# One early load put behind an activation, two warming products fewer, and three steps of the first items reordered

## The chip, the cores and the metric

The kernel runs on one core of one Trainium2 chip. The metric is the device time of one execution in microseconds, the median of several runs. A core has five engines that work in parallel, each through its own list of instructions in order: PE (matrix products, with its weight loads shown as PEld), DVE and ACT (elementwise work), POOL and SP (here they mostly issue DMAs). Semaphores hold an instruction back until another engine or a DMA has got far enough. All times below are in microseconds.

## The reference

The result is a gated mix of two branches over the same input x of 2048 rows and 512 columns, in float32:

```python
g = _sigmoid((x * gate_w).sum(-1, keepdims=True))
a = Re(DFT_seq(DFT_hidden(x)))          # four matrix products with cos/sin matrices
b = (silu(x @ w1) * (x @ w3)) @ w2      # 512 -> 1376 -> 512
return g * a + (1 - g) * b
```

Branch a is written with real and imaginary matrices: `a = x @ Wd_re.T`, `b = x @ Wd_im.T`, then `Ws_re @ a - Ws_im @ b`. The change touches only the start of the first half of branch b, `silu(x @ w1)` and `x @ w3`.

## The kernel before

**Products in three parts.** PE multiplies rounded float32 numbers. To keep the accuracy, each operand is split in two: `high` (line 107) rounds it on ACT, `low` (line 110) takes the rest on DVE, and `split` (line 113) does both. Each product then takes three matmuls: high by high, high by low, low by high (`mm3`, line 117, and `half`, line 420).

**Seven products in place of eight.** Most of the kernel multiplies 2 by 2 blocks with seven block products, which need sums of blocks. x^T is loaded as four blocks per half of the rows, B11, B21, B12 and B22 (`load_xo`, line 195, the tensor `xt`), and the sums T1 to T4 (`sum_xo`, line 205) are split like the blocks. For a weight chunk of 128 columns of w1 and w3, the raw load is `ws` (`load_w`, line 221); `wa` holds the split of its first three blocks, `wu` their four sums, and `wb` the split of these.

**Items.** The work of this stage is a list of items n = 0 to 20, each a weight chunk c and one half g of the rows. Item 0 is done by hand with eight plain block products into four PSUM banks C (lines 416 to 482), so that PE can start as soon as a single block of x and a single block of weights are there. From item 1 on `gate_up(n)` (line 337) does seven block products X, Y, Z. LOOK = 3: the first two products of item n + 3 are made while item n is worked on. For item n, `copy_x` copies X to `s1` on ACT, `sum_g` (line 296) adds Y on DVE, which completes the gate's sum and releases Y's bank (`bank(4 + n % 2)`), and `gate1` (line 301) takes the Silu of it on ACT, in place.

**Order.** The schedule is manual (line 399): each engine's list has the order of the calls in the code. Lines 440 to 501 write out the start by hand. Beside that there are tables `early`, `second`, `mid` and `at_end`, to which `do(table, n, f, ...)` (line 503) adds work that `gate_up(n)` runs at the named place: `early` behind the copy of X, `second` behind the copy of Z, `mid` behind the addition into u4, `at_end` last.

**The start.** SP issues, in this order, the first of four blocks of the first weights (`load_w(0, 0, 1)`, 128 KB), block B11 of x (512 KB), the other three blocks of the first weights (384 KB; the third load), then B21, B12, B22 and three more weight chunks (512 KB each). All of them stand in SP's one queue. Meanwhile DVE clears a small tile `warm`, and PE multiplies it by itself WARM = 11 times into a bank that nothing reads: these are the warming products. ACT's first activation, a Silu of 24 columns of `warm` into `act0` (line 407), loads the table of functions. `act0` is used later (line 923) in the same way for another table.

In item 0, C[0, 0] takes B11 and then B21, C[1, 0] the same with other weights; then C[0, 1] and C[1, 1] take B12 and B22. The Silu of C[0, 0] (line 455) stands ahead of the split of B22 (line 457) in ACT's list.

Of the kernel before, what the change touches and what calls it, by code (L numbers as in the profile page):

```python
# [9 lines left out]
AF = mybir.ActivationFunctionType  # L10
# [11 lines left out]
NG = NST // 2  # L22
NC = (F + P - 1) // P
NP2 = (NC + 1) // 2
WARM = 11
LOOK = 3
K = 9
W2_AT = (9, 11, 13, 15)
# [4 lines left out]
def fnet_swiglu_gate_kernel(  # L33
# [20 lines left out]
    nc = tc.nc  # L54
# [25 lines left out]
    def bank(k, name):  # L80
        return psum.tile([P, 512], F32, tag=f"ps{k}", name=name)
# [31 lines left out]
    def split(hi, lo, src):  # L113
        high(hi, src)
        low(hi, lo, src)
# [7 lines left out]
    act0 = const.tile([P, 24], F32, tag="act0", name="act0")  # L123
# [81 lines left out]
    def sum_xo(g, k, t):  # L205
        ST[g, k] = t
        nc.vector.tensor_sub(t, *(ST[g, v] for v in SUMS[k]))

    def xo_parts(g, k):
        o = XO[g][:, :, OPS.index(k)]  # L210
        return flat_x(o[:, 0]), flat_x(o[:, 1]), ST[g, k]

    def split_xo(g, k):
        split(*xo_parts(g, k))

    WS, WA, WB = {}, {}, {}
# [4 lines left out]
    def load_w(w, lo=0, hi=4):  # L221
        if lo == 0:
            WS[w] = f4_a.tile([P, 4, 256], F32, tag=f"f4_{4 + w % (LOOK + 1)}", name=f"ws{w}")
        nc.sync.dma_start(WS[w][:, lo:hi].rearrange("p a n -> p (a n)"),  # L224
                          w13[SETS[w], :, lo * 256 : hi * 256])
# [7 lines left out]
    def wa_parts(w, lo, hi):  # L233
        return (*(flat(WA[w][:, h, lo:hi]) for h in range(2)), flat(WS[w][:, lo:hi]))
# [47 lines left out]
    def copy_x(n, x):  # L282
        s1 = s1p.tile([P, 512], F32, tag="s1", name=f"s1_{n}")
        nc.scalar.activation(s1, x, AF.Copy)
        G[n] = (x, s1)
# [5 lines left out]
    def prod2(n):  # L291
        y = bank(4 + n % 2, f"Y{n}")
        prod(y, n, 1, 1, True)
        return y

    def sum_g(n, y):
        s1 = G[n][1]
        nc.vector.tensor_add(s1, s1, y)
        put_score(n, 0, s1)

    def gate1(n):
        nc.scalar.activation(G[n][1], G[n][1], AF.Silu)
# [3 lines left out]
    def put_score(n, j, gate):  # L306


        c, g = ITEMS[n]
        if c < NC - 1:  # L310
            return
        if not SC:
            SC[0] = wide("sc")
        p = F % P - 32 * g
        t = SC[0].rearrange("p (b n) -> p b n", b=2)
        nc.scalar.activation(t[p : p + 32, j], gate[F % P :], AF.Copy)
        if j == 1:
            nc.gpsimd.dma_start(gs[2 * g : 2 * g + 2].rearrange("b o n -> o b n"), t[p : p + 1])
            if g == 1:
                at_end.setdefault(n + 1, []).append(lambda: free(SC[0]))  # L320
# [10 lines left out]
    early, second, mid, at_end = {}, {}, {}, {}  # L331
# [70 lines left out]
    warm = s1p.tile([P, 1024], mybir.dt.bfloat16, tag="s1", name="warm")[:, :512]  # L402
    nc.vector.memset(warm, 0.0)
    wps = bank(7, "wps")
    for n in range(WARM):
        nc.tensor.matmul(wps, warm[:, :P], warm, start=True, stop=True)
    nc.scalar.activation(act0, warm[:, :24], AF.Silu)
    load_w(0, 1, 4)
    for k in ("B21", "B12", "B22"):
        load_xo(0, k)  # L410
# [7 lines left out]
    C = {(i, j): bank((0, 4, 6, 7)[2 * i + j], f"C{i}{j}") for i in range(2) for j in range(2)}  # L418

    def half(i, j, w, x, start):  # L420


        wp = lambda h, sl: a21[:, h, sl] if w is None else WA[0][:, h, w, sl]
        xp = lambda q, h: b12[:, h, q * 512 : (q + 1) * 512] if x is None else XO[0][:, h, x, q, :]
        for r in range(2):
            sl = slice(r * P, (r + 1) * P)
            for n, (u, v) in enumerate(((0, 0), (1, 0), (0, 1))):
                nc.tensor.matmul(C[i, j], wp(u, sl), xp(r, v), start=start and r == n == 0,  # L428
                                 stop=not start and r == 1 and n == 2)
# [5 lines left out]
    s1 = s1p.tile([P, 512], F32, tag="s1", name="s1_0")  # L435
# [16 lines left out]
        split(*xo_half("B21", q))  # L452
    half(0, 0, 1, 1, False)
    split(b12[:, 0], b12[:, 1], ST[0, "B12"])
    nc.scalar.activation(s1, C[0, 0], AF.Silu)
    half(1, 0, 2, 1, False)
    split_xo(0, "B22")
    half(0, 1, 0, None, True)
    WS.pop(0)
    load_w(4)  # L460
# [25 lines left out]
    y2 = prod2(2)  # L486
# [5 lines left out]
    low_wb(1)  # L492
    high(*xo_parts(0, "T3")[::2])
    y3 = prod2(3)
    sum_g(2, y2)
    copy_x(3, x3)
    low(*xo_parts(0, "T3"))
    new_wa(4)
    split(*wa_parts(4, 0, 3))
    gate1(2)  # L500
    sum_xo(0, "T4", ST[0, "B21"])

    def do(work, n, f, *a):
        work.setdefault(n, []).append(lambda: f(*a))
# [2 lines left out]
    do(early, 1, lambda: low(*xo_parts(0, "T1")))  # L507
    do(second, 1, lambda: split_xo(0, "T4"))
    do(second, 1, free, *(ST[0, b] for b in ("B11", "B21", "B12", "B22")))
    do(second, 1, sum_g, 3, y3)  # L510
    do(mid, 1, gate1, 3)


    for k in ("B11", "B21", "B12", "B22"):
# [426 lines left out]
    for p in range(KD):  # L941
        early = p < NG - NP2
# [71 lines left out]
```

## Time and profile before

| what | value |
|---|---|
| median of 3 runs | 711.14 (710.78 to 711.51) |
| the profiled execution, its own time | 710.82 |
| its span, first to last instruction | 709.1 |
| mean granted TensorE clock over the span | 0.999 |
| mean DMA rate over the span | 243 GB/s |
| SP's second load (B11), issue to landing | 4.14 |
| the third load, 384 KB, issue to landing | 4.6 |

The profile is one execution. Its page gives the busy time and the number of instructions of each engine, and the chain of work that ended last: followed back from the last instruction, at each step to what released it or to the instruction ahead of it on its engine. The timeline gives instructions in order of time, equal ones merged with their count; a merged row's length is the union of its instructions, whose last one ends later than the next can start, so spacings are read from starts. "SPq" is SP's issuing of DMAs, not the transfer.

### The profile page before, as it was taken

What the parts mean: (1) busy time and instruction counts of PE and PEld (TensorE: products, weight loads), DVE (VectorE), ACT (ScalarE), POOL (GpSimd) and SP (SyncE); (2) the same over time, 40 slices, a digit from 0 to 9 for tenths busy, and PEclk for the clock granted to TensorE, in tenths of its full rate; (3) what the DMA queues carried; (4) which work ended last, traced back from release to release, by engine and by line L of the source; (5) the groups of instructions that cost most, each with busy time, mean ns of one, the idle gap of its engine ahead of it and who ended that gap; (6) DMA issues with size and microseconds to landing.
All of it is one profiled execution on the core that took longest, in us unless ns stands there. A gap on an engine that the chain in (4) does not pass through costs nothing.

```text
span 709.1 us, 8596 instructions
## 1 busy us (share of the span) xinstructions
PE 703.6 (99%) x3089; PEld 578.5 (82%) x3089; DVE 605.1 (85%) x735; ACT 369.1 (52%) x479; POOL 64.0 (9%) x118
## 2 busy tenths in 40 slices
PE   9999999999999999999999999999999999999997
PEld 6788888888888888888888888888888888888886
DVE  6989988787679999887999589969997896897985
ACT  5665555655446754454554553544455455455451
POOL 0021111121110000000110001100110000000000
PEclk9999999999999999999999999999999999999999
DMA  7575556589997566712596238915999981773932
GB/s 281 201 290 214 209 193 251 186 311 355 421 410 269 221 193 241 293 60 89 175 361 251 90 121 296 370 49 189 379 419 415 358 272 56 296 285 135 321 120 89
DMA packets 45403, 172.54 MB, mean 243 GB/s; under 512 B 5296, under 2 KB 5424, under 8 KB 41520
## 3 DMA queue, kind: packets, MB, share of 16 engines
q1 hardware_dynamic: 32464, 118.50, 46.1%
q0 software_dynamic: 12608, 52.97, 18.8%
q8 instruction: 24, 0.39, 0.2%
q10 hardware_dynamic: 288, 0.52, 0.2%
q14 instruction: 19, 0.16, 0.1%
HBM read 114.82 MB, written 57.16 MB: 243 GB/s over the span
## 4 chain that ended last, share of the span: by engine, by line
PE 99%; DMA 1%; DVE 0%; ACT 0%; SPq 0%; issue 0%
PE P L119 69%; PE X L119 16%; PE Z L119 8%; PE Y L119 4%; PE C L428 2%; DMA xs_B<-xt 1%; DVE zc L807 0%; ACT xo L108 0%; SPq L224 0%
## 5 line engine op out<-in xcount | busy, mean ns | idle before, releaser
L119 PE MATMUL P<-zo,a 128*128 128x512 f32 x1344 | 305.5, 389 | 0.0
L119 PEld LDWEIGHTS P<-zo,a 128*128 128x128 f32 x1344 | 252.0, 188 | 53.3 <-DVE zo L111 1.1
L108 ACT ACTIVATE zo<-B 128x1024 fp32r<-128x1024 f32 (+1 forms) x182 | 189.3, 1045 | 184.5 <-PE P L119 96.4
L111 DVE TENSOR_TENSOR zo<-B,zo 128x1024 fp32r<-128x1024 f32 (+1 forms) x182 | 218.0, 1206 | 48.2 <-ACT zo L108 47.3
L119 PE MATMUL P<-zo,H 128*128 128x512 f32 x468 | 106.2, 389 | 0.0
L119 PEld LDWEIGHTS P<-zo,H 128*128 128x128 f32 x468 | 87.9, 188 | 18.2
L665 DVE TENSOR_TENSOR B<-B,B 128x1024 f32<-128x1024 f32 (+1 forms) x78 | 93.1, 1194 | 0.1
L119 PE MATMUL X<-xo,wb 128*128 128x512 f32 x378 | 93.1, 390 | 0.0
L119 PEld LDWEIGHTS X<-xo,wb 128*128 128x128 f32 x378 | 70.8, 188 | 15.4 <-DVE xo L111 0.5
L119 PE MATMUL P<-zo,Y 128*128 128x512 f32 x336 | 76.3, 389 | 0.0
L119 PEld LDWEIGHTS P<-zo,Y 128*128 128x128 f32 x336 | 63.1, 188 | 13.1
L327 POOL DMA_DIRECT2D hsp<-h x42 | 23.0, 548 | 128.4 <-DVE h L379 75.6
L119 PE MATMUL Z<-xo,wb 128*128 128x512 f32 x126 | 32.0, 389 | 0.0
L119 PE MATMUL X<-xo,wa 128*128 128x512 f32 x126 | 32.0, 389 | 0.0
L119 PE MATMUL Z<-xo,wa 128*128 128x512 f32 x126 | 32.0, 389 | 0.0
L119 PE MATMUL Y<-xo,wa 128*128 128x512 f32 x126 | 32.0, 389 | 0.0
L668 DVE TENSOR_TENSOR B<-B,B 128x1024 f32<-128x1024 f32 x26 | 31.8, 1221 | 0.0
L882 ACT ACTIVATE zu<-P 128x512 f32<-128x512 f32 x32 | 19.1, 598 | 20.3 <-PE P L119 20.3
L373 DVE TENSOR_TENSOR u<-u,X 128x512 f32<-128x512 f32 x21 | 14.4, 687 | 16.4 <-PE X L119 16.4
L119 PEld LDWEIGHTS Z<-xo,wb 128*128 128x128 f32 x126 | 23.6, 188 | 5.0
L119 PEld LDWEIGHTS Z<-xo,wa 128*128 128x128 f32 x126 | 23.6, 188 | 4.9
L119 PEld LDWEIGHTS X<-xo,wa 128*128 128x128 f32 x126 | 23.6, 188 | 4.9
(135 smaller groups left out, 550.5 us busy)
## 6 DMA issues: line engine op xcount, KB each, us to landing
B<-cc SPq DMA_DIRECT2D x64, 512.0 KB, 5.9
hsp<-h POOLq DMA_DIRECT2D x42, 256.0 KB, 3.7
B<-hsp SPq DMA_DIRECT2D x20, 512.0 KB, 10.3
wbsp<-wb POOLq DMA_DIRECT2D x8, 1024.0 KB, 4.3
wb<-wbsp SPq DMA_DIRECT2D x8, 1024.0 KB, 7.7
B<-zsp SPq DMA_DIRECT2D x16, 512.0 KB, 7.6
H<-w2sp SPq DMA_DIRECT2D x6, 1024.0 KB, 8.9
ws<-w SPq DMA_DIRECT2D x11, 512.0 KB, 4.8
```

Source lines behind the costliest of these rows:

```text
L108: nc.scalar.activation(hi, src, AF.Copy)
L111: nc.vector.tensor_sub(lo, src, hi.bitcast(F32))
L119: nc.tensor.matmul(ps, u, v, start=first and n == 0, stop=last and n == 2, skip_group_check=chain)
L327: nc.gpsimd.dma_start(hsp[g, b + k, j // 2, :, j % 2 * 512 : (j % 2 + 1) * 512], h)
L373: nc.vector.tensor_add(u4, u4, x)
L428: nc.tensor.matmul(C[i, j], wp(u, sl), xp(r, v), start=start and r == n == 0, stop=not start and r == 1 and n == 2)
L665: nc.vector.tensor_add(t, t, RAW[blk, b, q][:, :n])
L668: nc.vector.tensor_sub(t, RAW[blk, "B12", q], t)
L882: nc.scalar.activation(U[name][:, r], ps[r], AF.Copy)
```

## The change

It has three parts.

1. The first activation writes its 24 columns into the tile of the first weights, at the place that the third load will fill, in place of `act0`; `act0` gets a plain copy. Since the third load writes the same place, it has to wait for the activation, and SP's later loads stand behind it. WARM goes from 11 to 9.
2. The Silu of C[0, 0] moves behind the split of B22, that is, behind its high part in ACT's list.
3. The gate sum of item 2 (`sum_g(2, y2)` on DVE) and its Silu (`gate1(2)` on ACT) move from the written-out start into item 1, to the places that item 3's had, and those of item 3 move to item 2.

```diff
-WARM = 11
+WARM = 9
...
     wps = bank(7, "wps")
     for n in range(WARM):
         nc.tensor.matmul(wps, warm[:, :P], warm, start=True, stop=True)
-    nc.scalar.activation(act0, warm[:, :24], AF.Silu)
+
+    nc.scalar.activation(WS[0][:, 1, :24], warm[:, :24], AF.Silu)
+    nc.scalar.activation(act0, warm[:, :24], AF.Copy)
     load_w(0, 1, 4)
...
     split(b12[:, 0], b12[:, 1], ST[0, "B12"])
-    nc.scalar.activation(s1, C[0, 0], AF.Silu)
     half(1, 0, 2, 1, False)
     split_xo(0, "B22")
+    nc.scalar.activation(s1, C[0, 0], AF.Silu)
     half(0, 1, 0, None, True)
...
     y3 = prod2(3)
-    sum_g(2, y2)
     copy_x(3, x3)
     low(*xo_parts(0, "T3"))
     new_wa(4)
     split(*wa_parts(4, 0, 3))
-    gate1(2)
     sum_xo(0, "T4", ST[0, "B21"])
...
-    do(second, 1, sum_g, 3, y3)
-    do(mid, 1, gate1, 3)
+    do(second, 1, sum_g, 2, y2)
+    do(mid, 1, gate1, 2)
+    do(early, 2, sum_g, 3, y3)
+    do(mid, 2, gate1, 3)
```

## The prediction

> **What bounds the kernel now.** I read the profile's page first, then the chain of work that ended last.
>
> ```profile
> span 709.1 us, 8596 instructions
> PE 703.6 (99%) x3089; PEld 578.5 (82%) x3089; DVE 605.1 (85%) x735; ACT 369.1 (52%) x479; POOL 64.0 (9%) x118
> PE 99%; DMA 1%; DVE 0%; ACT 0%; SPq 0%; issue 0%
> ```
>
> PE is the bound from its first product to its last. So the change can gain only what makes PE start earlier or stop less often. The same chain in order of time (start, length) shows what stands ahead of PE:
>
> ```profile
> 1.18 4.14 DMA xs_B<-xt
> 5.35 0.43 ACT xo L108
> 5.82 11.44 PE C L428 x48
> ```
>
> The second load, B11, is issued at 1.18 and lands at about 5.33; ACT rounds its first piece, and the first real product starts at 5.82. The timeline gives the rest (start, length, engine, line, what, count, idle time before it and what ended it):
>
> ```profile
> 1.19 4.12 PE L406 MATMUL wps<-warm 128*128 128x512 bf16 x11 [1.19 <-DVE warm L403]
> 1.65 0.42 SPq L224 DMA_DIRECT2D ws<-w  x1
> 2.03 0.22 ACT L407 ACTIVATE act<-warm 128x24 f32<-128x24 bf16 x1
> 2.12 1.52 SPq L200 DMA_DIRECT2D xs_B<-xt  x3
> 3.15 0.42 ACT L108 ACTIVATE wa<-ws 128x256 fp32r<-128x256 f32 x1 [0.90 <-DMA ws<-w]
> 3.73 0.15 PEld L406 LDWEIGHTS <-warm 128*128 128x128 bf16 x1 [0.28 <-issue]
> 4.15 0.15 PEld L406 LDWEIGHTS <-warm 128*128 128x128 bf16 x1 [0.27 <-issue]
> 4.50 0.32 PEld L406 LDWEIGHTS <-warm 128*128 128x128 bf16 x2 [0.20 <-issue]
> 5.82 1.92 PE L428 MATMUL C<-xo,wa 128*128 128x512 f32 x6 [0.51 <-ACT xo L108]
> 7.01 0.42 DVE L111 TENSOR_TENSOR a<-ws,a 128x256 fp32r<-128x256 f32 x1
> 7.58 1.52 PE L428 MATMUL C<-xo,a 128*128 128x512 f32 x6
> 7.67 1.15 ACT L108 ACTIVATE xo<-xs_B 128x512 fp32r<-128x512 f32 x2 [0.46 <-DMA xs_B<-xt]
> 8.33 1.29 DVE L111 TENSOR_TENSOR xo<-xs_B,xo 128x512 fp32r<-128x512 f32 x2 [0.30 <-ACT xo L108]
> 8.94 2.88 PE L428 MATMUL C<-xo,wa 128*128 128x512 f32 x12
> 10.50 0.60 ACT L455 ACTIVATE s<-C 128x512 f32<-128x512 f32 x1 [0.51 <-PE C L428]
> 10.99 1.05 ACT L108 ACTIVATE xo<-xs_B 128x1024 fp32r<-128x1024 f32 x1
> 11.66 1.52 PE L428 MATMUL C<-b,wa 128*128 128x512 f32 x6
> 12.08 1.23 DVE L111 TENSOR_TENSOR xo<-xs_B,xo 128x1024 fp32r<-128x1024 f32 x1 [0.83 <-ACT xo L108]
> ```
>
> From 8.94 to 11.66 twelve products take 2.72, so one is 0.227 without a wait. B21, the fourth load, lands just before 7.67; its low half is ready only shortly before PE wants it. That is the second bound, right behind the first.
>
> **The early loads.** The stretches of the trace show PE, PEld, DVE, ACT, POOL, then the granted clock, the DMA share and GB/s:
>
> ```profile
> 0.74:1.70 0.96, 0.51 (x2) 0.24 (x3) 0.27 (x1) 0.96 (x1) 0.00 (x0) 1.00 0.00 0
> 3.00:4.00 1.00, 1.00 (x4) 0.33 (x3) 0.40 (x1) 0.42 (x1) 0.00 (x0) 1.00 0.98 349
> 4.00:5.00 1.00, 1.00 (x5) 0.35 (x3) 0.03 (x1) 0.00 (x0) 0.00 (x0) 1.00 1.00 368
> 5.00:6.25 1.25, 0.74 (x4) 0.30 (x2) 0.75 (x2) 0.90 (x2) 0.00 (x0) 1.00 0.93 341
> 6.25:7.64 1.39, 1.39 (x7) 0.92 (x6) 1.39 (x4) 0.96 (x3) 0.00 (x0) 1.00 1.04 410
> ```
>
> A load's data flows about 1.0 behind its issue (issued 0.74, nothing by 1.70), and from 3.00 on the DMA engines have no gap.
>
> *Third load.* It now waits for the activation that ends at 2.25 (2.03 + 0.22), so it is issued at about 2.3 instead of 1.65. All of SP's queue behind it, B21, B12, B22 and three weight loads, moves by the same 0.65. The extra 24-column copy (0.22) ends near 2.5, inside ACT's idle 0.90 before 3.15: nothing.
>
> B11's landing is the unknown. It keeps its issue at 1.18 and loses a competitor, so it cannot be later: lower end 0. Upper end: 524 KB at 410 GB/s behind the first load's landing (3.15) take 1.28, so 4.43, or 0.9 earlier. The third load still joins near 3.3 (2.3 + 1.0), which leaves it out of under half of the stretch from 2.7 to 5.33; I take 0.4.
>
> The Trainium skill, "DMA: Bandwidth & Descriptors", section "Queues, rings and completion order", speaks against this: on each DMA engine descriptors are consumed in ring order, so a later load of the same queue takes nothing from an earlier one. By that rule B11 lands when it did, and the sum would be 0 instead of a gain; no view here separates the 16 engines.
>
> B21's landing, now about 7.64: at the latest 0.65 later, the whole delay passed on. At the earliest: raising 3.00 to 6.25 to 410 GB/s returns 61 + 42 + 86 KB, or 0.46. The nearest row is the share of 0.93 to 1.04: a queue that is always busy doesn't care that B21 is issued at 2.77 when its turn comes near 6.36 (7.64 less 524 KB at 410). I take 0.1 earlier.
>
> *Warming products.* Their weight loads stand 0.42 apart up to 4.15, then 0.2: the products turn fast near 4.4, in the eighth of eleven. The two removed are fast ones, 0.22 each: PE is free near 4.9 instead of 5.3. It waits for B11 anyway, so by itself this is 0; it counts only if B11's first piece is ready before 5.3.
>
> *What PE gains.* With B11 0.4 earlier it starts at 5.42. The six products of B11 still take 7.58 - 5.82 = 1.76, since their waits for the splits move along. The next six need the low part at 7.01, which moves up with DVE. Then come B21's products. Their third needs B21's low half: 8.33 + 0.69 (half of the two, with an overlap; compare 0.68 for 512 columns below) = 9.02, and 0.06 for the hand-off. PE wanted it at 8.94 + 0.45 = 9.39, so only 0.31 of any earlier start survives. A stop costs some 0.1 more in refill (3.05 against 2.88 for twelve products, below), so 0.2 is left; with B21 0.1 earlier, **0.3**.
>
> *B22's high part ahead of the Silu.* B12 and B22 follow B21's 7.64 at 1.28 each, so B22 is there near 10.2. ACT sits idle 0.51 until 10.50 for C and rounds B22 only at 10.99. In the new order B22's high starts near 10.2, its low near 11.3, and DVE's idle 0.83 closes. The Silu ends near 11.8; its reader on DVE comes after B22's low and a sum (over 13). PE's first use of B22 is past 14, so by itself this is 0; without that cover it would cost 0.95 of ACT's time.
>
> *Two gate sums later.* This stage is where PE last stops:
>
> ```profile
> 24.77 0.68 DVE L298 TENSOR_TENSOR s<-s,Y 128x512 f32<-128x512 f32 x1
> 28.26 0.60 ACT L364 ACTIVATE u<-Z 128x512 f32<-128x512 f32 x1 [0.84 <-PE Z L119]
> 28.50 1.23 DVE L111 TENSOR_TENSOR xo<-t,xo 128x1024 fp32r<-128x1024 f32 x1
> 28.75 1.05 ACT L108 ACTIVATE xo<-xs_B 128x1024 fp32r<-128x1024 f32 x1
> 29.36 1.86 PE L119 MATMUL X<-xo,wb 128*128 128x512 f32 x6
> 29.84 1.23 DVE L111 TENSOR_TENSOR xo<-xs_B,xo 128x1024 fp32r<-128x1024 f32 x1
> 30.98 0.68 DVE L298 TENSOR_TENSOR s<-s,Y 128x512 f32<-128x512 f32 x1
> 31.07 1.53 PE L119 MATMUL Z<-xo,wa 128*128 128x512 f32 x6
> 33.05 0.68 DVE L373 TENSOR_TENSOR u<-u,X 128x512 f32<-128x512 f32 x1
> 33.79 3.05 PE L119 MATMUL X<-xo,wb 128*128 128x512 f32 x12
> 41.07 0.69 DVE L373 TENSOR_TENSOR u<-u,X 128x512 f32<-128x512 f32 x1 [0.73 <-PE X L119]
> ```
>
> PE loses 0.34 at 29.36 (1.86 against 1.52) to T1's low part at 28.50, and 0.17 at 33.79. With the sum of 24.77 gone, T1's low comes 0.68 earlier and the first stop ends. But T4's low (29.84) doesn't wait for DVE: it waits for T4's high on ACT (28.75 to 29.80), which stands behind the copy of Z at 28.26, and that one waits for PE. Behind T4's low come one gate sum, now the second instead of the third, four sums of weights, and the addition at 33.05 that frees X for PE. All of this keeps its distance from PE's Z. So PE arrives 0.34 sooner and waits at 31.1 and 33.8 instead: bounds 0 and 0.51 (0.34 + 0.17), value **0**.
>
> The third sum goes to the next item, where DVE idles 0.73 before 41.07: that covers its 0.68; uncovered it costs 0.68. The banks: Y of item 2 is read by 31.66, as Y of item 3 was, before PE rewrites that bank at 32.4.
>
> **The sum.** 0.3 + 0 + 0, against 710.82 of the profiled execution (span 709.1 and 1.7 around it). That lies 0.32 under the median of the three runs, so on the median: 711.14 - 0.3 = **710.8**.
>
> **Rivals.**
> - *Nothing moves* (B11 lands at 5.33). For: a DMA share near 1 throughout. Against: 349 to 368 GB/s, not 410, while both loads are under way. 711.1.
> - *The early stream comes forward whole.* B11 at 4.43 lets PE start near 4.9, 0.9 earlier. B21 must follow by 0.6 or more, beyond the 0.46 computed above; and both later stops must end, 0.51, if T4's chain has slack that I don't see. Together 1.4: 709.7.
> - *B21 becomes late, and the kernel slower.* The third load, at the low rates of 3.00 to 6.25, leaves the engines without work, and B21 inherits up to 0.65. Past 0.31 it decides: PE waits 0.65 - 0.31 + 0.1 = 0.45 at B21's products. 711.6. Against it: no gap in the DMA share, and over 2 us between B21's issue and its turn.
> - *PE turns fast later.* Nine products end warming near 4.9 and PE idles until B11 is there; if the turn came in that idle time's wake, each product until then would cost 0.2 more: 7 products from 5.8 are 1.4. 712.5. Against it: here the turn came at 4.4, before either removed product began. The granted-clock column reads 1.00 in all these stretches, so only the spacing tells.
>
> The Trainium skill, "TensorE: Matmul & The Clock Gate", Part 1, says that the clock is released after about 3.4 us of activity in a free-running window, so the turn may come later in another execution. The trace shows 3.2 from the first product (1.19) to the turn; the spread over executions isn't shown.
>
> **How the numbers follow.** Forecast 0.52, its own range 710.2 to 711.1 (0.1 to 0.7 gained, with the runs' scatter); nothing 0.16; whole stream 0.13; B21 late 0.11; late turn 0.08. The range runs from the whole stream's 709.7 to 711.7, just past B21's price, and leaves out the late turn and half of the whole stream. A change under 0.2% (1.42) can't be told from none by a measurement of this kernel. Faster by more: the far part of the whole stream and a little scatter, 0.12. Slower: the late turn and a little scatter, 0.10. Between: 0.78.
>
> **What would show it.** Right: the third load's issue at 2.3; B11's first rounding near 4.9; B21's products interrupted at their third; T1's stop at 29 gone and new ones at T4's low and the addition into u; the last product 0.3 earlier. Wrong: B11's rounding still at 5.35, B21's later than 7.95, or warming products 0.43 apart to the end.

## The result, and the profile after

| | median | lowest to highest | runs |
|---|---|---|---|
| before | 710.78 | 710.37 to 711.51 | 13 |
| after | 712.25 | 711.92 to 712.80 | 13 |

The ratio is 1.0023, with a 95% interval of 1.0016 to 1.0030: the change costs 1.47, and no run of the one kernel reaches into those of the other. The forecast was 710.8, so it is wrong, sign included. The profiled execution of after is the slowest of its 13, 712.80, and its span is 711.0 against 709.1.

The page of after, the span and the busy time of each engine:

```profile
span 711.0 us, 8593 instructions
PE 705.2 (99%) x3087; PEld 579.8 (82%) x3087; DVE 605.6 (85%) x735; ACT 369.4 (52%) x480; POOL 64.0 (9%) x118
```

Nothing there gives the loss away: PE is as full as before. The chain of waits of after in order of time (start, length, what) does:

```profile
1.18 4.37 DMA xs_B<-xt
5.57 0.42 ACT xo L108
6.04 13.21 PE C L430 x48
...
38.78 1.36 PE Z L119 x6
...
219.67 487.63 PE P L119 x2148
```

and here is the chain of before at the same places:

```profile
36.84 1.38 PE Z L119 x6
...
217.76 487.55 PE P L119 x2148
```

The 48 products of item 0 take 13.21 instead of the 11.44 of the prediction's rows, and start 0.22 later. These 1.99 are still 1.94 at the first Z of item 2 (38.78 against 36.84) and 1.91 at the last stage (219.67 against 217.76). So all of the loss lies in the first 20 us. The timeline of after there (start, length, engine, line, what, count, idle time before it and what ended it):

```profile
1.19 4.02 PE L406 MATMUL wps<-warm 128*128 128x512 bf16 x9 [1.19 <-DVE warm L403]
2.28 0.33 SPq L224 DMA_DIRECT2D ws<-w  x1
5.57 0.94 ACT L108 ACTIVATE xo<-xs_B 128x256 fp32r<-128x256 f32 x2 [2.01 <-DMA xs_B<-xt]
6.04 2.93 PE L430 MATMUL C<-xo,wa 128*128 128x512 f32 x6 [0.83 <-ACT xo L108]
7.64 0.42 ACT L108 ACTIVATE a<-ws 128x256 fp32r<-128x256 f32 x1 [1.13 <-DMA ws<-w]
8.77 2.33 PE L430 MATMUL C<-xo,a 128*128 128x512 f32 x6
9.00 1.15 ACT L108 ACTIVATE xo<-xs_B 128x512 fp32r<-128x512 f32 x2 [0.42 <-DMA xs_B<-xt]
10.93 2.88 PE L430 MATMUL C<-xo,wa 128*128 128x512 f32 x12
13.65 1.52 PE L430 MATMUL C<-b,wa 128*128 128x512 f32 x6
```

Two things are to be seen. First, the loads: the third is issued 0.63 later (2.28 against 1.65), but it comes in about 1.4 later (its rounding on ACT starts at 7.64; before, the load landed near 6.25, 4.6 behind its issue), and B21's rounding starts at 9.00 against 7.67. The delay isn't just handed on, it has doubled. B11, whose issue didn't move, isn't a bit earlier (5.57 against 5.35).

Second, the clock: B11's six products take 2.93 against 1.92 and the next six 2.33 against 1.52, though no wait is shown ahead of the second group. From 6.04 to 8.77 one of six takes 0.46, from 10.93 to 13.65 one of twelve takes 0.227, half of that. PE turns fast near 10.4 here, against 4.4 before.

The stretches of after show PE, PEld, DVE, ACT, POOL, then granted clock, DMA share and GB/s:

```profile
4.00:5.00 1.00, 1.00 (x3) 0.15 (x1) 0.02 (x1) 0.00 (x0) 0.00 (x0) 1.00 0.58 208
5.00:6.25 1.25, 0.42 (x2) 0.21 (x2) 0.53 (x2) 0.68 (x2) 0.00 (x0) 1.00 0.95 256
6.25:7.64 1.39, 1.39 (x4) 1.07 (x5) 1.07 (x2) 0.26 (x1) 0.00 (x0) 1.00 1.08 360
```

From 4 to 5, where before moved 368 GB/s at a share of 1.00, after moves 208 at 0.58; the two stretches behind it are slower too. The row of loads has got a hole that it hadn't.

The later stage of after, in the timeline:

```profile
31.81 1.23 DVE L111 TENSOR_TENSOR xo<-xs_B,xo 128x1024 fp32r<-128x1024 f32 x1 [1.06 <-ACT xo L108]
32.69 1.82 PE L119 MATMUL Z<-xo,wa 128*128 128x512 f32 x6
33.09 1.00 PEld L119 LDWEIGHTS Z<-xo,wa 128*128 128x128 f32 x5 [0.43 <-DVE xo L111]
35.75 1.22 PEld L119 LDWEIGHTS X<-xo,wb 128*128 128x128 f32 x6 [0.29 <-DVE u L373]
35.75 3.03 PE L119 MATMUL X<-xo,wb 128*128 128x512 f32 x12
```

The stop at T1's low part is gone, a new one stands at T4's low (Z of 1.82), and the one at the addition into u is still there (3.03 for the twelve products; 3.05 before). Nothing is gained on balance, as forecast.

So one profile holds two suspects, late loads and a late turn of the clock, and both delay the same products. Which of them costs the 1.47 of the median can't be read from it.

### The profile page after: what moved, and what is told of

Its sections match the earlier page's. It is cut to its first block, busy times and chain, and to the rows that moved or that the text cites. A ratio compares the mean times of both kernels' runs of the same rounds, so it can differ in the third digit from the quotient of the medians.

```text
span 711.0 us, 8593 instructions
## 1 busy us (share of the span) xinstructions
PE 705.2 (99%) x3087; PEld 579.8 (82%) x3087; DVE 605.6 (85%) x735; ACT 369.4 (52%) x480; POOL 64.0 (9%) x118
## 4 chain that ended last, share of the span: by engine, by line
PE 99%; DMA 1%; DVE 0%; ACT 0%; SPq 0%; issue 0%
PE P L119 69%; PE X L119 16%; PE Z L119 8%; PE Y L119 4%; PE C L430 2%; DMA xs_B<-xt 1%; DVE zc L809 0%; ACT xo L108 0%; SPq L224 0%
## 5 line engine op out<-in xcount | busy, mean ns | idle before, releaser
L119 PEld LDWEIGHTS Y<-xo,wa 128*128 128x128 f32 x126 | 23.6, 188 | 4.9
```

The source lines that it names most:

```text
L119: nc.tensor.matmul(ps, u, v, start=first and n == 0, stop=last and n == 2, skip_group_check=chain)
```

## The experiments

Eleven kernels were run, each beside the kernel before on the same chip. The table of all of them stands first. "Issue" is the third load's; the next three columns are where ACT starts to round B11, the third load and B21 (before: 5.35, 6.28, 7.67), from the timelines; then GB/s and DMA share between 4 and 5; then how long the warming products last from 1.19; then where the last stage (P) starts in the chain of waits. These are of the one profiled execution of each kernel, which need not lie at its median; the last two columns compare all runs, eleven of each kernel (13 of after).

| kernel | issue | B11 | third | B21 | GB/s, share | warming | P from | less before | ratio, 95% interval |
|---|---|---|---|---|---|---|---|---|---|
| before | 1.65 | 5.35 | 6.28 | 7.67 | 368, 1.00 | 4.12 (11) | 217.76 | | |
| after | 2.28 | 5.57 | 7.64 | 9.00 | 208, 0.58 | 4.02 (9) | 219.67 | +1.47 | 1.0023 [1.0016, 1.0030] |
| load_wait_only | 2.28 | 5.12 | 6.92 | 8.28 | 241, 0.99 | 4.79 (11) | 218.12 | +1.14 | 1.0015 [1.0006, 1.0024] |
| warm9_only | 1.65 | 5.17 | 6.12 | 8.11 | 380, 0.96 | 4.02 (9) | 218.01 | -0.02 | 1.0002 [0.9993, 1.0011] |
| order_only | 1.66 | 4.96 | 6.26 | 7.66 | 350, 0.96 | 4.49 (11) | 217.56 | -0.17 | 0.9994 [0.9985, 1.0003] |
| after_warm11 | 2.28 | 4.98 | 7.81 | 9.12 | 274, 0.77 | 4.78 (11) | 219.05 | +1.13 | 1.0016 [1.0008, 1.0025] |
| wait_no_delay | 1.66 | 5.00 | 6.16 | 7.85 | 372, 1.01 | 4.88 (11) | 217.79 | +0.06 | 1.0000 [0.9991, 1.0009] |
| delay_short | 2.22 | 5.71 | 7.18 | 8.49 | 224, 0.72 | 4.87 (11) | 218.34 | +1.54 | 1.0020 [1.0010, 1.0029] |
| delay_long | 3.79 | 5.02 | 7.54 | 9.03 | 77, 0.31 | 4.40 (11) | 218.95 | +1.16 | 1.0016 [1.0007, 1.0025] |
| warm6 | 1.66 | 5.00 | 6.36 | 7.61 | 370, 1.02 | 2.74 (6) | 218.59 | +1.34 | 1.0017 [1.0008, 1.0025] |
| delay_least | 1.83 | 4.97 | 6.23 | 7.96 | 386, 1.03 | 4.63 (11) | 217.80 | +0.67 | 1.0005 [0.9995, 1.0015] |
| b21_late | 1.65 | 4.83 | 5.83 | 7.60 | 401, 1.04 | 4.88 (11) | 217.78 | +0.28 | 1.0008 [0.9999, 1.0016] |
| after_no_wait | 1.66 | 5.25 | 6.31 | 7.57 | 389, 1.09 | 4.02 (9) | 219.61 | -0.04 | 1.0001 [0.9993, 1.0010] |

### The parts one at a time

**load_wait_only**: the first part of the change without the fewer warming products.

```diff
-    nc.scalar.activation(act0, warm[:, :24], AF.Silu)
+    nc.scalar.activation(WS[0][:, 1, :24], warm[:, :24], AF.Silu)
+    nc.scalar.activation(act0, warm[:, :24], AF.Copy)
```

> The kernel before, with only the third load put behind the first activation; 11 warming products, old order. Theory of the dry queue (the late third load leaves DMA engines without work, B21 lands near 9.0 instead of 7.6 and PE waits at B21's products): slower by 0.9 to 1.2 us, B21's first rounding at 8.8 to 9.1, the DMA share of 4 to 5 us well under 0.9. Theory of the clock alone (the loss comes from nine warming products and PE's idle time behind them): within 0.3 us of before. Theory of the order (the gate sums or B22's place cost it): within 0.3 us.

Measured: 712.0 against 710.86. The wait alone carries some 1.1 of the loss. Its profiled execution is the lowest of its runs (P only 0.36 later), yet the late loads are there: the third 0.64 later, B21 0.61. That is less than the dry queue asked for (B21 at 8.8 to 9.1), and so is the gap in the share: 0.99 from 4 to 5, with the rate down to 241 GB/s all the same.

**warm9_only**: only the number of warming products.

```diff
-WARM = 11
+WARM = 9
```

> The kernel before, with only 9 warming products in place of 11. Theory of the clock: whenever the turn to fast products has not come by about 5 us, PE's idle time ahead of B11 puts it off to 8 to 11 us, which costs 1.1 to 1.8 us in those executions and nothing in the others: median slower by 0.5 to 1.5 us, with a wider scatter than before (over 1.2 us from the fastest to the slowest). Theory of the dry queue alone: within 0.3 us. Loads land as before in either case (B21's first rounding at 7.5 to 7.8).

Measured: 710.84 against 710.86, no change in the median. But its eleven runs aren't of one kind: nine lie from 710.37 to 711.01, two at 712.61 and 712.79. The pair is taken up under after_no_wait.

**order_only**: the second and third part (B22's split ahead of the Silu, the gate sums later), with 11 warming products and no wait.

```diff
     split(b12[:, 0], b12[:, 1], ST[0, "B12"])
-    nc.scalar.activation(s1, C[0, 0], AF.Silu)
     half(1, 0, 2, 1, False)
     split_xo(0, "B22")
+    nc.scalar.activation(s1, C[0, 0], AF.Silu)
...
-    do(second, 1, sum_g, 3, y3)
-    do(mid, 1, gate1, 3)
+    do(second, 1, sum_g, 2, y2)
+    do(mid, 1, gate1, 2)
+    do(early, 2, sum_g, 3, y3)
+    do(mid, 2, gate1, 3)
```

> The kernel before, with only the order changed (B22's high part ahead of the Silu, two gate sums later). Prediction's step: the stop of 0.34 at T1's low part goes and comes back as stops at T4's low part and at the addition into u; within 0.3 us of before. Theory that the order costs the time: slower by 1 us or more, with stops of that size on PE between 20 and 45 us.

Measured: 710.69 against 710.86, which is no change. Its timeline:

```profile
5.42 1.93 PE L428 MATMUL C<-xo,wa 128*128 128x512 f32 x6
8.58 3.04 PE L428 MATMUL C<-xo,wa 128*128 128x512 f32 x12
9.07 2.13 PEld L428 LDWEIGHTS C<-xo,wa 128*128 128x128 f32 x10 [0.30 <-DVE xo L111]
...
30.50 1.82 PE L119 MATMUL Z<-xo,wa 128*128 128x512 f32 x6
30.90 0.99 PEld L119 LDWEIGHTS Z<-xo,wa 128*128 128x128 f32 x5 [0.43 <-DVE xo L111]
```

Its second half repeats after's stop at T4's low. Its first half happens to show what the prediction wanted from the load's wait. B11 came early in this execution (4.96), PE started 0.40 earlier, was stopped at B21's third product by the low part on DVE, and kept 0.20 at the last stage (217.56 against 217.76).

**after_warm11**: after with 11 warming products, so the wait and the new order.

```diff
-WARM = 9
+WARM = 11
```

> The changed kernel, but with 11 warming products. Dry queue: slower than before by 0.9 to 1.2 us, like the load's wait alone, since B21 at 9.0 is what PE waits for as long as the turn comes by about 8 us. Clock alone: back at before, within 0.3 us. Both acting, but hiding behind each other: slower than before by 0.9 to 1.2 us, and 0.2 to 0.6 us under the changed kernel.

Measured: 711.99 against 710.86, as load_wait_only. This profiled execution (span 710.3) lies near its median, and its products run at the fast pace from B11's six on, so it shows the late loads by themselves. Its chain of waits and its timeline:

```profile
2.28 5.51 DMA ws<-w
7.79 0.02 issue
7.81 0.42 ACT a L108
8.24 0.04 issue
8.28 10.29 PE C L430 x42
...
219.05 487.54 PE P L119 x2148
```

```profile
5.50 1.88 PE L430 MATMUL C<-xo,wa 128*128 128x512 f32 x6
8.28 1.88 PE L430 MATMUL C<-xo,a 128*128 128x512 f32 x6 [0.90 <-ACT a L108]
9.12 1.16 ACT L108 ACTIVATE xo<-xs_B 128x512 fp32r<-128x512 f32 x2 [0.38 <-DMA xs_B<-xt]
9.79 1.29 DVE L111 TENSOR_TENSOR xo<-xs_B,xo 128x512 fp32r<-128x512 f32 x2 [0.32 <-ACT xo L108]
10.00 3.13 PE L430 MATMUL C<-xo,wa 128*128 128x512 f32 x12
12.96 1.53 PE L430 MATMUL C<-b,wa 128*128 128x512 f32 x6
```

The chain no longer runs through B11 but through the third load, 5.51 from issue to landing. PE starts 0.32 before the kernel before did, has its six products done by 7.38, stands 0.90 until the third load is rounded, and reaches B21's products at 10.00 instead of 8.94. B21's low stops it again (3.13 for twelve), so it is 1.30 late at 12.96 (before: 11.66), and 1.29 at the last stage.

The 0.90 isn't what sets these 1.30. From the start of B21's low on DVE to the products behind B21's twelve pass 3.17 here (9.79 to 12.96). They are 3.16 in load_wait_only (8.95 to 12.11), 3.14 in delay_short and delay_long below (9.16 to 12.30 and 9.70 to 12.84), and 3.14 in order_only (8.32 to 11.46), where nothing was late and PE didn't wait for the third load. So in all of these PE is held until B21's low part is there, and would be without the stop of 0.90; what the late third load costs, it costs through B21, the next load behind it. The chain can't show this, as it merges the 42 products into one row.

### Is it the wait, the delay, or the later B21?

**wait_no_delay**: the third load waits, but for something long done: DVE clears the 24 columns right behind `warm`.

```diff
     nc.scalar.activation(act0, warm[:, :24], AF.Silu)
+    nc.vector.memset(WS[0][:, 1, :24], 0.0)
     load_w(0, 1, 4)
```

> The kernel before, and the third load waits for DVE, which clears 24 columns of the place that the load fills; that is done by about 1.4, ahead of the load's usual issue at 1.65. So there is a wait and no delay. Theory that the lateness costs the time: third load issued at 1.65 to 1.7, median within 0.3 us of before, B21's first rounding at 7.5 to 8.1. Rival, the waiting form of the load is itself slower (its descriptors come later, whatever the time of issue): slower by 0.9 to 1.2 us, like the wait for the activation, B21 at 8.2 or later.

Measured: 710.76 against 710.70. A wait as such costs nothing; the issue stays at 1.66 and the share at 1.01.

**delay_short, delay_long and delay_least**: the same, with 3, 7 and 2 full clears of the tile's second block, so that the issue comes at 2.22, 3.79 and 1.83.

```diff
     nc.scalar.activation(act0, warm[:, :24], AF.Silu)
+    for _ in range(3):
+        nc.vector.memset(WS[0][:, 1, :], 0.0)
     load_w(0, 1, 4)
```

> The same with three clearings of 256 columns: the third load is issued near 2.0 to 2.1, some 0.4 late in place of 0.63. Theory of the dry queue with the delay passed on and slack of 0.2 to 0.3 at B21's products: slower by 0.2 to 0.9 us. If only a delay past a threshold counts (above 0.5): within 0.2 us. Rival, the form of the wait: 0.9 to 1.2 us, like the others.

> The same with seven clearings: the third load is issued near 3.2 to 3.3, about 1.6 late. Dry queue: B21's first rounding at 9.0 to 10.2, slower by 1.3 to 2.2 us, more than the 1.1 of the delay by 0.63. B11, alone in the queue until past 4.2, lands at 4.3 to 4.8 if the third load ever took transfer time from it, and at 4.9 to 5.5 as in all runs so far if it did not (the loads of one queue go in order on each DMA engine).

> The kernel before with two clearings of 256 columns ahead of the third load: it is issued near 1.85 to 1.95, some 0.2 to 0.3 late. So far a wait without delay cost nothing and delays of 0.57, 0.63 and 2.13 cost 1.54, 1.14 and 1.16 us: a step, no slope. If the step lies below 0.2 (any break in the row of issues): slower by 0.9 to 1.5 us. If it lies between 0.3 and 0.57: within 0.3 us.

Measured: the issue was 0.57, 2.13 and 0.17 late, not quite what was aimed at with the first two; the medians are +1.54, +1.16 and +0.67. The last has an interval that includes none, but 7 of its 11 runs lie from 711.15 to 711.68, above all of the 27 runs of the kernel before (at most 711.09) but one of 714.14; so a delay of 0.17 seems to cost something already. The profiled executions of delay_short (711.40) and delay_least (710.92) are among the lowest of their runs. So the loss comes with the delay and without the activation. It isn't in proportion: nearly four times the delay costs no more, where the delay passed on would have cost 1.3 to 2.2. A stretch and a part of the chain of delay_long:

```profile
4.00:5.00 1.00, 1.00 (x4) 0.30 (x2) 0.04 (x1) 0.00 (x0) 0.00 (x0) 1.00 0.31 77
```

```profile
3.79 3.73 DMA ws<-w
7.51 0.02 issue
7.54 0.42 ACT a L108
...
218.95 487.61 PE P L119 x2148
```

Here SP has nothing in the queue behind B11 until 3.79, and the engines are idle for most of the stretch from 4 to 5 (0.31, 77 GB/s). B11 nevertheless lands where it does in the other kernels, its rounding at 5.02. The third load then needs only 3.73, against 5.51 when it was issued 1.51 sooner (after_warm11), so both land at nearly the same time. (In load_wait_only, issued at 2.28 too, it was in by 6.9; the executions differ.)

**b21_late**: the third load on time, but B21, the next in the queue, waits for six clears of a part of its own tile.

```diff
-    for k in ("B21", "B12", "B22"):
+    ST[0, "B21"] = wide("xs0_B21")
+    for _ in range(6):
+        nc.vector.memset(ST[0, "B21"][:, :256], 0.0)
+    nc.sync.dma_start(ST[0, "B21"], xt[0, XRAW.index("B21")])
+    for k in ("B12", "B22"):
         load_xo(0, k)
```

> The kernel before, with the break in the row of issues moved one load on: the third load goes out at 1.65 as ever, but B21 waits for six clearings of part of its place and is issued near 3.2, 1.1 late; its data may flow from about 4.2, 0.7 ahead of its turn near 4.9 (the same margin that the third load had in the changed kernel: 2.28 + 1.0 against 4.0). Theory that a load costs time only if it is issued too late for its turn by the 1.0 of the first load: within 0.3 us, B21's first rounding by 8.1. Theory that a load issued behind a break starts slowly on some engines whenever it comes this close to its turn: B21's first rounding at 8.3 or later, slower by 0.5 to 1.5 us.

Measured: 710.92 against 710.64, the interval just includes none. In the profiled execution (710.87) B21 is issued at 3.39 instead of 2.12, twice the delay of the change, and its rounding starts at 7.60, no later than before. The rate falls here too, but later and less (289 GB/s from 6.25 to 7.64 against 410), and what comes later is B12, the next load (rounded at 9.11 against 8.93). Four of its eleven runs, from 711.77 to 712.18, stand apart from the other seven (at most 711.06). The profile is one of the seven, so why the four are slower is open.

### The clock

**warm6**: five warming products fewer, nothing else.

```diff
-WARM = 11
+WARM = 6
```

> The kernel before with 6 warming products: they end near 3.8, and PE idles for 1.5 to 2 us until B11 is rounded. Theory of the clock: the turn to fast products is counted from the products' restart in nearly every execution, so it comes at 8 us or later and the kernel is slower by 1.0 to 2.5 us, with the spread of the late turn. If the turn needs only some 3.2 us after the first product, with or without idle time between: within 0.3 us of before.

Measured: 712.04 against 710.70. The loads are on time (5.00, 6.36, 7.61), so this is the clock alone. PE in its timeline:

```profile
1.19 2.74 PE L406 MATMUL wps<-warm 128*128 128x512 bf16 x6 [1.19 <-DVE warm L403]
5.46 2.93 PE L428 MATMUL C<-xo,wa 128*128 128x512 f32 x6 [1.53 <-ACT xo L108]
8.19 1.76 PE L428 MATMUL C<-xo,a 128*128 128x512 f32 x6
```

After 1.5 of idle time PE is slow until some way into the second six: a turn near 8.6.

**after_no_wait**: the whole change but for the wait, so 9 warming products and the new order.

```diff
-    nc.scalar.activation(WS[0][:, 1, :24], warm[:, :24], AF.Silu)
-    nc.scalar.activation(act0, warm[:, :24], AF.Copy)
+    nc.scalar.activation(act0, warm[:, :24], AF.Silu)
```

> The changed kernel without the wait: 9 warming products and the new order, the third load issued at 1.65. If the wait alone carries the loss: within 0.3 us of before at the median, with a few executions some 1.8 us slower, as with 9 products alone. If nine products and the new order together cost something that each alone does not: slower by 0.5 us or more at the median.

Measured: 710.60 against 710.64. Taking the wait out of after gives all of the loss back. Ten of its eleven runs end by 711.11, and one takes 712.70; this is the profiled one. Its timeline:

```profile
5.72 2.93 PE L428 MATMUL C<-xo,wa 128*128 128x512 f32 x6 [0.51 <-ACT xo L108]
6.31 0.42 ACT L108 ACTIVATE a<-ws 128x256 fp32r<-128x256 f32 x1
7.57 1.15 ACT L108 ACTIVATE xo<-xs_B 128x512 fp32r<-128x512 f32 x2 [0.32 <-DMA xs_B<-xt]
8.44 2.52 PE L428 MATMUL C<-xo,a 128*128 128x512 f32 x6
10.80 2.89 PE L428 MATMUL C<-xo,wa 128*128 128x512 f32 x12
```

All loads are on time, and PE is slow to 10.5 all the same: a late turn costs 1.85 here (P at 219.61). In the profiled execution of after, with the same late turn and the loads 1.3 to 1.4 late, P starts at 219.67. The two costs don't add: the slow products end so late that the late loads are there by then.

## Why the prediction was wrong

- **The third load's issue at 2.3**: right, 2.28.
- **B21 "0.1 earlier", and "at the latest 0.65 later"**: this is the step that failed, in sign and in its bound. B21's rounding is 0.61 to 1.45 later where the third load is late by 0.57 or more at its issue. The argument was that a busy queue doesn't care when B21 is issued. For B21 itself that holds in the one execution that shows it: b21_late issues it 1.27 later and it lands on time. The queue didn't stay busy because the load ahead of B21 was late, and the "no gap in the DMA share" that spoke against the rival was read from the kernel before, which is no proof that none would open. In after's stretches (rates above against those of before, from 4.00 to 7.64) 160 + 106 + 70 KB less are moved, which at 410 GB/s is 0.82 of B21's 1.33. The rest doesn't show in sums over the 16 engines.
- **The third load's own landing**: the same mistake at its root. The prediction let it "join near 3.3" and from then on counted its bytes as moving. The runs show it landing 0.64 to 1.53 later than before (roundings at 6.92 to 7.81 against 6.28), and B21's rounding follows it by 1.31 to 1.49 in all of these (before: 1.39), so B21 takes over the lateness. In after_warm11 PE also stands 0.90 for the third load at C[1, 0], which no term had; but B21's low part holds PE for longer, so this adds nothing.
- **B11 "0.4 earlier"**: wrong, 0. Where the third load is late its rounding starts at 4.98 to 5.71, where not at 4.83 to 5.35. delay_long, with nothing else in the queue until 3.79, has it at 5.02, so the third load took nothing from B11. The Trainium skill, "DMA: Bandwidth & Descriptors", section "Queues, rings and completion order", has it that each DMA engine consumes descriptors in ring order, from which the prediction had worked out the same. The trace agrees (5.02).
- **The rival "B21 becomes late"**: right, at 0.11, in the mechanism, the place and the rule of its price; only its lateness was mis-sized, with the whole delay passed on, 0.65, as the worst case. Its rule, the lateness less 0.31 of slack plus 0.1 of refill, gives 0.40, 0.61, 1.15 and 1.24 with the measured lateness of B21 in load_wait_only, delay_short, delay_long and after_warm11 (0.61, 0.82, 1.36 and 1.45). Their last stages start 0.36, 0.58, 1.19 and 1.29 later. By this rule the loss of the median, some 1.1 with the late load alone, stands for a B21 about twice as late as the third load's issue (an estimate), as in after_warm11, whose profiled execution (712.12) lies near its median.
- **What an early start would bring (0.2)**: right by the one execution that had it (order_only), but the wait doesn't bring it.
- **Two warming products at nothing**: right for the median (710.84), for the wrong reason. "Here the turn came at 4.4, before either removed product began" took one execution's turn for the kernel's. Eleven slow products 0.427 apart would fill 4.7 from 1.19, and the table's column shows 4.12 before but 4.40 to 4.88 in every other kernel with eleven: in most of these executions the turn comes only at the end of the warming or behind it. With nine, 2 of 11 runs and 1 of 11 took 1.8 to 2.1 more; of the 106 runs of the kernel before, two lie that high (713.07 and 714.14).
- **The rival "PE turns fast later"** (0.08): its time of 712.5 is near what such an execution takes (712.70 in after_no_wait; the two high runs of warm9_only, 712.61 and 712.79, have no profile), and after's profile is one. But it isn't what makes the median: after_no_wait has nine products too and loses nothing. after is 0.26 slower than after_warm11 (712.25 and 711.99, not run side by side); late turns may add this, but the intervals don't tell the two apart.
- **B22 ahead of the Silu, and the gate sums**: right, nothing, with the stops where they were said to be (the one at the addition was there before, too).

What stays open: why a third load issued 0.6 late, still 2.7 ahead of B11's landing, comes in slowly at all. In load_wait_only the engines are busy at a share of 0.99 from 4 to 5 and move 241 GB/s; in delay_long they are mostly idle. So there isn't one picture of an empty queue that covers both, and why the loss doesn't grow beyond a delay of 0.57 isn't explained either. No version beat the kernel before: order_only's ratio includes 1.

## What to carry to other kernels

When a change delays one DMA, cost that load's own landing and, from it, the landings of the loads behind it, and don't take the delay as their upper bound: here 0.6 at the issue became 0.6 to 1.5 at the landings. Then ask which landing holds the reader last; a wait that ends earlier costs nothing, however long it is. A DMA share near 1 in the profile before says that the queue is fed as it is issued now, not that it has time to spare. A state read from one execution, such as when the clock turns, needs a second one before a step is costed on it.

## What the runs showed of the hardware

- Delaying the third load of this row of back-to-back loads doesn't cost in proportion: 0, 0.17, 0.57, 0.63 and 2.13 of delay at the issue cost 0.06, 0.67 (its interval includes none), 1.54, 1.14 and 1.16.
- The turn of the products from 0.43 to about 0.22 apart varies from run to run and depends on what PE does until then. Unbroken warming gave the lengths of 4.12 to 4.88 above. Behind nine products, a pause of 0.42 was followed by a turn near 7 (warm9_only: its first six products take 2.17 to the start of the next), and pauses of 0.51 and 0.83 by one near 10.5, some 5 after the pause began; 1.5 behind six put it to 8.6. The Trainium skill, "TensorE: Matmul & The Clock Gate", Part 1, has it that the window of about 3.4 is free-running. The spread over executions agrees with this.
- The granted-clock column reads 1.00 for all stretches above, those with products 0.43 apart included. In these stretches only the spacing of the products shows the turn.
